# Attention and a gated feed-forward for one token: two weight loads cut into three transfers each by partitions

## The chip, the cores and the metric

One Trainium2 chip, one core of it. The metric is the time of the program on the device in microseconds (us), as a median of several executions. Beside it there is one profiled execution, which gives the trace. All times "at x us" are counted from the start of the profile's span.

## What is computed

One token `x` (512 values, bf16) goes through two branches that are mixed by a gate:

```python
g = sigmoid((x * gate_w).sum(-1, keepdims=True))
a = A_ref(x, k_cache, v_cache, wq, wo)   # attention, 32 query heads, 8 KV heads,
                                         # 32768 cached positions, head size 128
b = (silu(x @ w_gate) * (x @ w_up)) @ w_down     # 512 -> 1792 -> 512
return g * a + (1 - g) * b
```

`A_ref` projects `x` with `wq` (512 x 4096), takes scores against all cached keys of the KV head, softmax, the weighted sum of the values, and projects with `wo` (4096 x 512). The two caches hold 64 MiB each; with the weights some 148 MB have to be read once.

## The kernel before, in words

**Pages.** SBUF holds five pages of 32 KB per partition (`page`, L155). A cache page is half the positions of one KV head: 16384 positions x 128 values, 128 positions on each partition, 4 MB in one transfer of 128 partitions x 32,768 bytes. Keys use pages 0 and 2 (`PG_K`), values 1 and 3 (`PG_V`). Page 4 first holds `wq`, and at the end `wo`. Page 3 (`PG_F`) first holds `w_gate` and `w_up` side by side (`wgu`, L200): 128 partitions, for each weight four rows of 1792 values, which is 14,336 bytes per partition and weight.

**Queue.** All loads are issued by SyncE (SP) on one DMA queue (q1), in the order written out in its block (L259 to L312): `wq` (L279), the two rows of 1 KB (`x` L280, `gate_w` L281), `w_gate` and `w_up` (L283, in a loop over both), key pages 0 and 1 of the first head, value page 0, and from there on keys and values in turn (L262). Before a page is loaded again, SP waits until its reader is done: `sem_fill` for keys (L269), `sem_v_free` for values (L274). The second value page of the first head goes where the two weights lie, so SP waits there for `sem_pe_h` (L276), which TensorE (PE) raises after it has read the weights. At the end come the last value pages, `w_down` (L305) and `wo` in five transfers cut along its rows (L300).

A transfer raises its semaphore by 16 in all when it has landed, in parts as the DMA engines (16 of them) finish their shares. `sem_f` belongs to `w_gate` and `w_up` together: PE waits for 32 (L354).

**TensorE.** After the wait for `x` and the projection with `wq` (L334, 128 matmuls), PE waits for `sem_f` and multiplies both weights with `x` (L358, 112 matmuls). Then a loop over heads: for each key page, eight units of eight 128x128 transposes into PSUM (L372), copies by VectorE (L637), and score matmuls (L384); values of the head before are multiplied with the exponentials between (L429). ScalarE takes the exponentials (L540) after GpSimd's maximum over partitions (L254). At the end `w_down` and `wo` are multiplied with the results (L441, L453), the row is copied out of PSUM (L682), and SP and ScalarE store one half each, two rows of 256 bytes (L205).

**What the change touches**: the loop at L282 to L285 and the number in the wait at L354. The lines that the prediction's steps touch besides are L262 (page loads), L276 (SP's wait for PE), L358 and L372 (PE's work behind the wait), and L300, L453 and L682 (the end).

Of the kernel before, what the change touches and what calls it, by code (L numbers as in the profile page):

```python
# [13 lines left out]
def bass_gated_mix__gqa_block_cached__swiglu_ffn__decode_kernel(  # L14
# [23 lines left out]
    KC = D // 128  # L38
# [20 lines left out]
    WO_CUTS = [0, 8, 18, 26, 30, 32]  # L59
    KW = 1  # L60
    WD_CUT = 8
    WIDE = WO_CUTS[KW + 1]
    OC = NOUT // 128

# [12 lines left out]
    with ExitStack() as es:  # L77
        def S_(name):
            return es.enter_context(nc.semaphore(name))
# [3 lines left out]
        sem_f = S_("s_f")  # L83
# [46 lines left out]
        def T(name, shape, dt):  # L130
            return es.enter_context(nc.sbuf_tensor(name, shape, dt))
# [40 lines left out]
        O2 = T("O2", [128, WOJ], BF16)  # L172
        O2z = T("O2z", [128, WOJ - WIDE, SW], BF16)
        part = T("part", [128, NOUT], FP32)
# [25 lines left out]
        wgu = page[:, PG_F, 0 : 2 * KC * F].rearrange("p (w c f) -> p w c f", w=2, c=KC)  # L200
        wo_v = page[:, PG_X, 0 : WOJ * NOUT].rearrange("p (j n) -> p j n", j=WOJ)

        def store(eng, k):
            n = RPS * 128
            eng.dma_start(  # L205
                out[0, 0, n * k : n * (k + 1)].rearrange("(c n) -> c n", c=RPS),
                res_row[64 * k + SW - 1 : 64 * k + SW + 1, :],
            ).then_inc(sem_out, 16)

        with nc.Block("main") as block:  # L210
# [48 lines left out]
            @block.sync  # L259
            def _(sp):  # L260
                def cache(which, g, b, p, sem):
                    sp.dma_start(  # L262
                        page[:, p, :].rearrange("p (r d) -> p r d", d=DH),
                        which[0, g, b * BLK : (b + 1) * BLK, :].rearrange("(p r) d -> p r d", r=R),
                    ).then_inc(sem, 16)

                def load_k(g, b):
                    if g:
                        sp.wait_ge(sem_fill, UPG * (g - 1) + UPP * (b + 1))  # L269
                    cache(A_k_cache, g, b, PG_K[b], sem_page[PG_K[b]])  # L270

                def load_v(g, b):
                    if g:
                        sp.wait_ge(sem_v_free, NB * (g - 1) + b + 1)  # L274
                    elif PG_V[b] == PG_F:
                        sp.wait_ge(sem_pe_h, 1)  # L276
                    cache(A_v_cache, g, b, PG_V[b], sem_page[PG_V[b]])

                sp.dma_start(wq_v, A_wq.rearrange("(p c) n -> p c n", c=KC)).then_inc(sem_q, 16)  # L279
                sp.dma_start(x_row[0:1, :], A_x[0, :, :]).then_inc(sem_ld_x, 16)  # L280
                sp.dma_start(gw_row[0:1, :], gate_w.unsqueeze(0)).then_inc(sem_ld_x, 16)  # L281
                for w, src in enumerate((B_w_gate, B_w_up)):  # L282
                    sp.dma_start(  # L283
                        wgu[:, w, :, :], src.rearrange("(p c) f -> p c f", c=KC)
                    ).then_inc(sem_f, 16)  # L285
                for b in range(NB):
                    load_k(0, b)
                load_v(0, 0)
                load_k(1, 0)
                load_v(0, 1)  # L290
                load_k(1, 1)
                for g in range(2, G):
                    for b in range(NB):
                        load_k(g, b)
                        load_v(g - 1, b)

                def load_wo(k):
                    a, b = WO_CUTS[k], WO_CUTS[k + 1]
                    src = A_wo.rearrange("(p j) n -> p j n", j=WOJ)
                    sp.dma_start(wo_v[:, a:b, :], src[:, a:b, :]).then_inc(sem_wo[k], 16)  # L300

                load_v(G - 1, 0)
                sp.wait_ge(sem_fill, UPG * (G - 1) + UPP)
                cache(A_v_cache, G - 1, 1, PG_K[0], sem_page[PG_K[0]])
                sp.dma_start(  # L305
                    wd[:, :, :], B_w_down.rearrange("(p j) n -> p j n", j=FC)
                ).then_inc(sem_ld_wd, 16)
                sp.wait_ge(sem_pe_q, 1)
                for k in range(len(sem_wo)):
                    load_wo(k)  # L310
                sp.wait_ge(sem_dve_row, 1)
                store(sp, 0)  # L312

            @block.tensor
            def _(pe):
                pe.wait_ge(sem_ld_x, 32)
                pe.wait_ge(sem_const, 1)
                for src, base in ((x_row, M_X0), (gw_row, M_X0 + KC)):
                    srcv = src[0:1, :].rearrange("o (p c) -> o c p", c=KC)
# [31 lines left out]
                    )  # L351
                ins.then_inc(sem_pe_qp, 1)

                pe.wait_ge(sem_f, 32)  # L354
                for w, base in enumerate((M_G0, M_U0)):
                    for j in range(FC):
                        for c in range(KC):
# [81 lines left out]
                def emit_wide(w, vec, j, first, last):  # L439
                    c = j % NSTRIP  # L440
                    return pe.matmul(  # L441
                        ps_w[32 * c : 32 * c + 1, :],
                        vec[:, j : j + 1],
                        w[:, j, :],
                        start=first,
                        stop=last,
                        skip_group_check=True,
                    )

                def emit_rows(lhs, rhs, first, last):  # L450
                    for oc in range(OC):
                        e = oc % RPS
                        ins = pe.matmul(  # L453
                            ps_c[32 * oc : 32 * oc + (1 if e else SW), 0:128],
                            lhs(e),
                            rhs[:, oc * 128 : (oc + 1) * 128],
                            start=first,
                            stop=last,
                            skip_group_check=True,
                        )  # L460
                    return ins

                def emit_end():
# [11 lines left out]
                    pe.wait_ge(sem_psw, 1)  # L475
                    for j in range(WD_CUT):
                        emit_wide(wd, tT, j, j < NSTRIP, False)
# [5 lines left out]
                    for k, s in enumerate(sem_wo):  # L483
                        if k == 1:
                            for j in range(WD_CUT, FC):
                                emit_wide(wd, tT, j, False, False)
                        pe.wait_ge(s, 16)
                        for j in range(WO_CUTS[k], WO_CUTS[k + 1]):
                            if j < WIDE:
                                ins = emit_wide(wo_v, O2, j, False, j >= WIDE - NSTRIP)  # L490
                            else:
                                ins = emit_rows(
                                    lambda e: O2[:, j : j + 1] if e else O2z[:, j - WIDE, :],
                                    wo_v[:, j, :],
# [70 lines left out]
            def _(dve):  # L565
# [67 lines left out]
                with dve.Fori(0, G * STEP, STEP) as i:  # L633
# [42 lines left out]
                dve.tensor_copy(  # L676
                    O2z[:, :, SW - 1], ps_m[:, M_O0 + WIDE : M_O0 + WOJ]
                ).then_inc(sem_dve_oz, 1)
# [32 lines left out]
```

## Time and profile before

| what | us |
|---|---|
| time, median of 3 runs (range) | 352.69 (352.42 to 352.89) |
| the profiled execution | 352.48 |
| its span, first to last instruction | 350.7 |
| PE busy | 269.5 (77%) |
| VectorE (DVE) busy | 176.9 (50%) |
| ScalarE (ACT) busy | 32.1 (9%) |
| q1, share of 16 DMA engines | 98.5% |
| read from HBM | 148.11 MB, 422 GB/s over the span |
| `w_gate`, issue to landing | 15.4 |
| `w_up`, issue to landing | 20.6 |
| K pages, issue to landing (median) | 27.2 |

How to read it: the shares of busy time are averages over the whole span. The page has a line with the busy tenths of the DMA engines in 40 slices, one with GB/s, and one for each queue. The view of waits names the engine that waited, for whom, us in total, times and the longest. The chain of work is followed backwards from the last instruction, and each step names what released it. The timeline lists instructions of one line merged, with the idle time before them and what ended it. Beside these views the trace keeps a record of every DMA packet (queue, start, duration, bytes; not which of the 16 DMA engines) and of every increment that a landing transfer gives to its semaphore.

### The profile page before, as it was taken

Reading aid. Unit: us, or ns where it says so; the run is one execution under the profiler, and the core shown is the slowest. Engines: PE = TensorE matmul, PEld = TensorE weight load, DVE = VectorE, ACT = ScalarE, POOL = GpSimd, SP = SyncE. Lnnn points to the kernel's source line nnn. Section 1 sums busy time; section 2 is a strip of 40 time slices with the busy share of each in tenths; the row PEclk is TensorE's granted clock in tenths of the full one; section 3 lists DMA queues with packets and bytes.
Section 4 is the critical chain, followed back from the end, with each engine's and each line's share of the span. In section 5 each row is a group of like instructions: output and inputs, shape, how many; then the busy total and the mean of one; then the engine's idle time right before and its main releaser. Section 6 shows DMA issues by size and latency. Waiting matters only on the chain.

```text
span 350.7 us, 8919 instructions
## 1 busy us (share of the span) xinstructions
PE 269.5 (77%) x4005; PEld 232.4 (66%) x4005; DVE 176.9 (50%) x193; ACT 32.1 (9%) x148; POOL 6.9 (2%) x29
## 2 busy tenths in 40 slices
PE   0446987898999959796797949696898959795584
PEld 0446987887796939495785839394876849493232
DVE  0010878474783928365472828175653819184011
ACT  1000000500030040002100040003000040004000
POOL 4000000000000000000000000000000000000000
PEclk9999989696998999889696989679886969679565
DMA  8999999999999999999999999999999999999995
GB/s 329 418 448 417 437 430 439 418 430 426 445 434 422 430 431 441 430 430 422 445 434 426 430 426 445 430 426 426 441 437 426 426 430 445 430 426 426 422 419 218
DMA packets 5925, 148.25 MB, mean 423 GB/s; under 512 B 666, under 2 KB 668, under 8 KB 924
## 3 DMA queue, kind: packets, MB, share of 16 engines
q1 hardware_dynamic: 5912, 148.12, 98.5%
q8 instruction: 7, 0.11, 0.1%
q14 instruction: 2, 0.02, 0.0%
q10 hardware_dynamic: 4, 0.00, 0.0%
HBM read 148.11 MB, written 0.00 MB: 422 GB/s over the span
## 4 chain that ended last, share of the span: by engine, by line
DMA 64%; PE 31%; DVE 2%; SPq 1%; issue 1%
DMA page<-in_A_k_cache_dram 53%; PE pst L372 23%; DMA page<-in_A_wo_dram 11%; PE ps_sc L384 5%; DVE ktT L637 2%; PE ps_o L429 1%; PE pst L453 1%; PE pst L441 0%; PE ps_m L410 0%; SPq L283 0%; SPq L262 0%; DVE part L680 0%; SPq L305 0%; SPq L300 0%; SPq L279 0%
## 5 line engine op out<-in xcount | busy, mean ns | idle before, releaser
L637 DVE COPY ktT<-pst 128x2048 bf16<-128x2048 bf16 x128 | 156.1, 1224 | 106.5 <-PE pst L372 99.4
L372 PE MATMUL pst<-ident_f,page 128*128 128x128 f32 x1024 | 160.2, 315 | 40.2 <-DMA page<-in_A_k_cache_dram 38.8
L372 PEld LDWEIGHTS pst<-ident_f,page 128*128 128x128 f32 x1024 | 137.2, 164 | 50.6 <-DMA page<-in_A_k_cache_dram 46.7
L384 PEld LDWEIGHTS ps_sc<-qcur,ktT 128*128 128x128 bf16 x2048 | 67.0, 97 | 11.4 <-DVE ktT L637 10.0
L384 PE MATMUL ps_sc<-qcur,ktT 128*128 128x8 bf16 x2048 | 67.9, 166 | 8.6 <-DVE ktT L637 8.6
L429 PE MATMUL ps_o<-page,ET 128*16 128x512 bf16 x512 | 42.1, 487 | 4.6 <-DMA page<-in_A_v_cache_dram 4.6
L429 PEld LDWEIGHTS ps_o<-page,ET 128*16 128x16 bf16 x512 | 13.3, 104 | 23.2 <-issue 10.7
L531 ACT ACTIVATE nbias<-gmax 128x4 f32<-128x4 f32 x8 | 1.6, 205 | 263.6 <-POOL gmax L254 263.6
L540 ACT ACTIVATE ET<-ps_sc,nbias 128x128 bf16<-128x128 f32 x64 | 23.9, 554 | 0.6
L540 ACT ACTIVATION_READ_ACCUMULATOR ET<-ps_sc,nbias 128x1 f32 x64 | 18.2, 284 | 0.0
L642 DVE TENSOR_REDUCE pmaxf<-ps_sc 128x4 f32<-128x512 f32 x16 | 11.1, 691 | 11.5 <-PE ps_sc L384 11.5
L410 PE MATMUL ps_m<-sel,acc 128*128 128x4 f32 x72 | 10.8, 273 | 3.7 <-ACT acc L552 3.7
L410 PEld LDWEIGHTS ps_m<-sel,acc 128*128 128x128 f32 x72 | 10.1, 217 | 4.3 <-ACT acc L552 4.3
L358 PE MATMUL ps_m<-xT,page 128*128 128x1 bf16 x112 | 6.9, 198 | 4.8 <-DMA page<-in_B_w_up_dram 4.8
L321 PE MATMUL ps_m<-ones_bf,x_row 1*128 1x1 bf16 x4 | 0.3, 174 | 13.1 <-DMA gw_row<-in_gate_w_dram 13.1
L358 PEld LDWEIGHTS ps_m<-xT,page 128*128 128x128 bf16 x112 | 6.8, 162 | 4.9 <-DMA page<-in_B_w_up_dram 4.9
L254 POOL PARTITION_ALL_REDUCE gmax<-pmax x8 | 3.0, 373 | 302.7 <-DVE pmax L644 302.7
L321 PEld LDWEIGHTS ps_m<-ones_bf,x_row 1*128 1x128 bf16 x4 | 0.2, 116 | 13.1 <-DMA gw_row<-in_gate_w_dram 13.1
L552 ACT ACTIVATE acc<-ps_o 128x512 f32<-128x512 f32 x8 | 5.2, 653 | 13.6 <-PE ps_o L429 13.6
L660 DVE RECIPROCAL rS<-pst 128x32 f32<-128x32 f32 x1 | 0.4, 359 | 12.1 <-PE pst L465 12.1
L577 DVE CAST xT<-ps_m 128x4 bf16<-128x4 f32 x1 | 0.2, 163 | 12.1 <-PE ps_m L321 12.1
L616 DVE TENSOR_TENSOR t<-sg,ps_m 128x14 f32<-128x14 f32 x1 | 0.2, 170 | 10.7 <-ACT sg L525 10.7
(65 smaller groups left out, 38.4 us busy)
## 6 DMA issues: line engine op xcount, KB each, us to landing
page<-in_A_k_cache_dram SPq DMA_DIRECT2D x16, 4096.0 KB, 27.2
page<-in_A_v_cache_dram SPq DMA_DIRECT2D x16, 4096.0 KB, 31.1
page<-in_A_wq_dram SPq DMA_DIRECT2D x1, 4096.0 KB, 12.2
page<-in_A_wo_dram SPq DMA_DIRECT2D x2, 1024.0 KB, 38.8
page<-in_B_w_gate_dram SPq DMA_DIRECT2D x1, 1792.0 KB, 15.4
page<-in_B_w_up_dram SPq DMA_DIRECT2D x1, 1792.0 KB, 20.6
wd<-in_B_w_down_dram SPq DMA_DIRECT2D x1, 1792.0 KB, 34.5
page<-in_A_wo_dram SPq DMA_DIRECT2D x1, 1280.0 KB, 39.1
```

The costliest lines, as they stand in the source:

```text
L254: pool.partition_all_reduce(gmax[:, g, :], pmax[:, g * STEP : g * STEP + HPG], 128, ReduceOp.max).then_inc(sem_gmax, 1)
L358: ins = pe.matmul(ps_m[:, base + j : base + j + 1], wgu[:, w, c, :].rearrange("d (p j) -> d j p", j=FC)[:, j, :], xT[:, c : c + 1], start= ...
L372: ins = pe.transpose(pst[u % NST][:, k * 128 : (k + 1) * 128], kv[:, n * 128 : (n + 1) * 128], ident_f[:, :],)
L384: ins = pe.matmul(ps_sc[b][:, col : col + 2 * HPG], kt[:, k, e, :], qcur[:, e, :], start=(e == 0), stop=(e == 1),)
L410: ins = pe.matmul(ps_m[:, M_P0 : M_P0 + HPG], acc[:, q, :], sel4[:, q * HPG : (q + 1) * HPG], start=(q == 0), stop=(q == RQ - 1),)
L429: ins = pe.matmul(ps_o[32 * c : 32 * c + RQ * HPG, :], ET[:, n : n + RQ, :].rearrange("p n h -> p (n h)"), view[:, k * RQ : (k + 1) * RQ, ...
L453: ins = pe.matmul(ps_c[32 * oc : 32 * oc + (1 if e else SW), 0:128], lhs(e), rhs[:, oc * 128 : (oc + 1) * 128], start=first, stop=last, sk ...
L531: act.activation(nbias[:, g, :], gmax[:, g, :], ACT.Copy, scale=-SCALE).then_inc(sem_nbias, 1)
L540: act.activation(ET[:, b * R : (b + 1) * R, h], sc[:, h, :], ACT.Exp, bias=nbias[:, g, h : h + 1], scale=SCALE, accum_out=esum[:, g, b, h ...
L552: act.activation(acc[:, :, :].rearrange("p q d -> p (q d)"), ps_o[:, :], ACT.Copy).then_inc(sem_acc, STEP)
L637: dve.tensor_copy(ktT[:, u % NKT, :], pst[u % NST][:, :].bitcast(BF16)).then_inc(sem_cp, 1)
L642: dve.tensor_reduce(pmaxf[:, b, :], sc, AX.X, ALU.max).then_inc(sem_pmax, 4)
```

## The change

Each of the two weights is loaded in three transfers instead of one, cut by partitions: `w_gate` in 0 to 111, 112 to 123 and 124 to 127 (112, 12 and 4 partitions), `w_up` in 0 to 111, 112 to 119 and 120 to 127 (112, 8 and 8). They stand in the same place in SP's order, the bytes of each partition and their destination are the same, and each transfer raises `sem_f` by 16, so PE waits for 96 instead of 32. Nothing else changes.

```diff
+    FFN_CUTS = ((0, 112, 124, 128), (0, 112, 120, 128))
...
                 for w, src in enumerate((B_w_gate, B_w_up)):
-                    sp.dma_start(
-                        wgu[:, w, :, :], src.rearrange("(p c) f -> p c f", c=KC)
-                    ).then_inc(sem_f, 16)
+                    srcv = src.rearrange("(p c) f -> p c f", c=KC)
+                    for a, b in zip(FFN_CUTS[w], FFN_CUTS[w][1:]):
+                        sp.dma_start(wgu[a:b, w, :, :], srcv[a:b, :, :]).then_inc(sem_f, 16)
...
-                pe.wait_ge(sem_f, 32)
+                pe.wait_ge(sem_f, 16 * sum(len(c) - 1 for c in FFN_CUTS))
```

One line is added near the top, and the loop keeps its length, so that a line of the changed kernel is one further down than in the kernel before (L358 is L359); the loads of the two weights are at L286.

## The prediction

> **What bounds the kernel now.** I read the page from its second part down: the slices, the queues, the chain. Then the waits, the windows and the timeline, and last the records behind them, of single DMA packets and landings.
>
> From the page: the busy tenths and rates of the DMA queues, the queue that carries the data, and the chain that ended last.
>
> ```profile
> DMA  8999999999999999999999999999999999999995
> GB/s 329 418 448 417 437 430 439 418 430 426 445 434 422 430 431 441 430 430 422 445 434 426 430 426 445 430 426 426 441 437 426 426 430 445 430 426 426 422 419 218
> ...
> q1 hardware_dynamic: 5912, 148.12, 98.5%
> q8 instruction: 7, 0.11, 0.1%
> ...
> DMA 64%; PE 31%; DVE 2%; SPq 1%; issue 1%
> ```
>
> The transfers never pause. 148.12 MB go through q1 at one rate, and PE's 31% of the chain lies between DMA landings that released it.
>
> The waits (us in total, times, longest) say the same: PE waits for K pages, hardly for anything else.
>
> ```profile
> PE pst L372 <- DMA page<-in_A_k_cache_dram: 38.8, 13, 4.6
> ...
> PE ps_m L358 <- DMA page<-in_B_w_up_dram: 4.8, 1, 4.8
> ```
>
> The last windows column is GB/s, the one before it the DMA share:
>
> ```profile
> 103.00:303.00 200.00, 164.06 (x2424) 141.88 (x2422) 111.85 (x110) 18.08 (x90) 1.86 (x5) 0.84 1.00 432
> ```
>
> 432 over 16 is 27.0 GB/s for one DMA path (one of the 16 engines with its ring). The packet records refine this: each path starts a 32,768 B packet every 1.210 us and a 14,336 B packet every 0.532 us, to some ns, from the fifth packet of a path to the end. These are 27.1 and 26.9 GB/s. When one path stalls the others do not speed up: **the limit is per path, not one pool.** A path that falls behind stays behind.
>
> How far apart they are, the landing records tell: the last w_o transfer's sixteen increments come from 346.17 to 348.15 us. Against the first, eight paths lie at 0 to 0.53, two at 0.89 and 1.04, six at 1.59 to 1.98 us. The cause is in the packet records: six paths stood for 0.93 to 1.09 us each, while a 16 KB instruction packet (q8) went through, and two others for 0.31 us (8 KB). The latest path sets the end; the last matmul starts at 348.19, and the last copy follows:
>
> ```profile
> 304.64 39.11 DMA page<-in_A_wo_dram
> ...
> 348.65 0.29 DVE res_row L682
> ```
>
> The span is 350.7 us and this execution's time 352.48, so 1.78 us lie around it; the median of the runs shown is 352.69, 0.21 more. I add to 352.48.
>
> **The change, part by part.** Bytes, partitions and matmuls stay. What changes is which path writes which row (one row is 14,336 B for one partition). Before, 128 rows are 8 for each path, twice: 16. How are small transfers spread? The packet records have two cases: the x row and the gate row (one partition) are one 1,024 B packet each, both on the same path, and a store of two partitions is two packets starting 5 ns apart, hence on two. So I take an even division and the same paths first: 112 rows as 16x7, 12 as 12x1, 4 as 4x1, 8 as 8x1. Call the paths 0 to 15. Rows for both weights: paths 0 to 3 get 7+1+1+7+1+1 = 18; 4 to 7 get 7+1+7+1+1 = 17; 8 to 11 get 15; 12 to 15 get 14. By the count alone that is +1.06, +0.53, -0.53 and -1.06 us (rows by 0.532). The trace does not number its paths: of 0 to 3 only the x row's path is known to be an early one.
>
> *Issue on SP.* Two issues of 0.36 and 0.53 us become six. Four more by 0.23 to 0.53 (SP's rows of the head) are 0.9 to 2.1, say 1.5 us, by which the first K issue moves from 2.79. Cost 0: q1 is busy with w_q until 12.4 us. Without that cover it would cost the 1.5. There are 32 more semaphore packets (16+12+4+16+8+8 = 64 for 32) of 9 ns, at most 4 more on a path: 0.04 us.
>
> *PE's wait* is one wait as before, now for 96. Behind it stand the 112 matmuls of L358 and then the K transposes:
>
> ```profile
> 22.84 6.88 PE L358 MATMUL ps_m<-xT,page 128*128 128x1 bf16 x112 [4.84 <-DMA page<-in_B_w_up_dram]
> ...
> 32.86 5.16 PE L372 MATMUL pst<-ident_f,page 128*128 128x128 f32 x24 [3.13 <-DMA page<-in_A_k_cache_dram]
> ```
>
> If the weights land late, so does the K page behind them on the same rings, and the 3.13 us of idleness between the two groups stay about as they are. The V load that waits for sem_pe_h stands on SP behind a K load issued at 44.62, 15 us after the matmuls end. Cost 0 beside the path's own delay.
>
> *The rows themselves.* Here lies the price. In every transfer of before, a path writes eight partitions that no other path writes, so the trace cannot say whether the 27 GB/s belong to the path or to the partitions it writes to. The change separates them: four transfers put 12, 4, 8 and 8 paths on the last 16 partitions, which are two paths' worth of rows by any even share. Lower bound: sharing costs nothing, a row is 0.532. Upper: the partitions of one share take 27 GB/s whoever writes; with four paths in one share a row takes 4x0.532 = 2.13 us, with eight 4.26. I take **four to a share**, the smaller reading, between the ends; the rows nearest to it are the instruction packets: through the same paths, to another destination, 16 KB took 0.946 to 1.107 us, 15 to 17 GB/s. A path's pace depends on where it writes.
>
> Paths 0 to 3 then need 14x0.532 + 4x2.13 = 15.97 us where they needed 16x0.532 = 8.51: +7.5. Shares of seven rows do not line up with shares of eight either, so in each 112-row transfer a path meets another about once: one row doubled, 2x0.53 = +1.1 (from 0 to twice that). The share's own path, ahead by then with its K page, writes there too: a fifth writer for part of the four rows, estimated at half of 4x0.53, or +1.1 (from 0 to 2.1). Sum +9.7 on the slowest of paths 0 to 3. The end is set by the latest path, and these may have had a lead of up to 1.98; with eight of sixteen late I take off 1.2. **Net +8.5: 352.48 + 8.5 = 361.0 us.** Small readings of all three (7.5 - 1.98) give 358.0, large ones (7.5+2.1+2.1) 364.2. Eight to a share wherever more than four rows go: three rows at 4.26, one at 2.13, 7.45+14.9-8.5 = +13.9, the far end, 366.4.
>
> [...]
>
> **The rivals.**
> 1. *The pace belongs to the path, and the late paths are 8 to 15* (not slower). For it: identical pace whatever the size or source. Against: nothing ever tried two writers. The late ones shed 0.53 or 1.06; the first four arrive at no later than about 0.53+1.06 = 1.6 instead of 1.98: -0.4, 352.1 us. It needs early paths at 0 to 3 and decides only if sharing costs them under 0.4 us in all.
> 2. *The pace belongs to the path, but a late one is among the first four:* 1.98+1.06, so +1.1, 353.5 us. Eight late paths of fifteen make this as likely as the first, if they do not lie in a row.
> 3. *Sharing is partial*, as when a share takes two writers at full pace: a row 1.06, four rows +2.1, two extra rows +1.06 included in the count: 14x0.532+4x1.06-8.51 = +3.2, with meetings up to +5: 356 us.
> 4. *The 112 rows go out one row to each path in turn*, so that all sixteen stand on two or four shares at once: 14 rows at 2.13 are 30 for 7.5, over +20: 375 us.
>
> That the change does nothing at all is excluded unless small transfers are spread over all sixteen paths; the two small cases above speak against it.
>
> **How the numbers follow.** Forecast 0.70, rivals 0.13, 0.07, 0.07 and 0.03. The forecast gets most since a path's pace was seen to change with its destination, and since the change puts four writers and more where only one ever wrote; rivals 1 and 2 share 0.20 because the even pace is explained by the path as well. Under 0.2% (0.7 us) this kernel cannot be told from no change. Faster by that: 0.03, as perfect evenness of the sixteen (mean 1.0 behind the first, latest 1.98) is worth only 1.0 us. Within: 0.12, the rest of the first rival and some of the second. Slower: 0.85. The range, 353.0 to 365.0, holds rivals 2 and 3 and the forecast but for its far end: 8 in 10.
>
> **What would show it.** q1 with 5944 packets; w_up's landing (22.8 us before) at 30 to 33 and the first K page (32.8) at 41 to 43, the sixteen increments of a K page then spread over 6 us or more instead of 2; everything after it shifted by about 8.5, with PE's waits for K pages unchanged in sum to some us. A first K page at 33 to 34 with the old spread means rivals 1 or 2, and I am wrong on sharing; w_up past 45 means rival 4. Rows of 14,336 B with 2.1 us in the packet records prove the step, rows of 0.53 disprove it.

## The result, and the profile after

The changed kernel takes 363.62 us (median of 6, 362.84 to 364.67), the kernel before 352.61 (median of 6): a ratio of 1.0315, 95% interval 1.0304 to 1.0326, or **+11.0 us**. The forecast was slower, 361.0 in 353.0 to 365.0. The profiled execution has a span of 361.8 us, 11.1 more than before. Of the executions behind this document one, of the near kernel below, took 1136.2 us and is left out of its ratio.

The page of the changed kernel, the lines that answer to those shown of before: DMA slices and rates, the queue, the chain.

```profile
DMA  8999999999999999999999999999999999999993
GB/s 344 318 219 288 422 433 429 429 427 428 442 420 442 420 438 428 435 428 435 435 424 438 424 438 428 435 428 438 431 424 442 424 442 420 435 431 435 416 417 159
...
q1 hardware_dynamic: 5944, 148.12, 98.2%
...
DMA 65%; PE 30%; DVE 2%; SPq 1%; issue 1%
```

The busy line is as full as before, and so is q1's share. The line below tells the two kernels apart: slices 2 to 4 move 318, 219 and 288 GB/s where they moved 418, 448 and 417. So a path counts as busy also while its bytes move at half the rate (the windows below have a share of 1.02 at 216 GB/s). From slice 5 on the rates are the old ones.

The windows view of the changed kernel puts that in stages (last two columns: DMA share, GB/s).

```profile
12.10:17.50 5.40, 3.99 (x136) 3.83 (x136) 0.92 (x6) 0.20 (x1) 0.39 (x1) 1.00 1.03 295
17.50:33.00 15.50, 0.21 (x2) 0.14 (x2) 1.23 (x6) 0.00 (x0) 0.00 (x0) 1.00 1.02 216
33.00:43.00 10.00, 7.04 (x113) 6.96 (x114) 0.40 (x2) 0.18 (x1) 0.00 (x0) 1.00 1.00 428
103.00:303.00 200.00, 161.13 (x2413) 141.27 (x2412) 112.86 (x113) 21.76 (x108) 2.23 (x6) 0.86 1.00 432
```

The first row is the first 112-partition transfer, the second the rest of the weights, half of the usual 432. The long stretch in the middle has the same 432 as before: what is lost is lost by about 33 us (but for 1.0 us on the latest path, below), and it is never won back.

TensorE in the timeline: the matmuls with the two weights start at 33.40 instead of 22.84, and the first K page 9.99 later than before. Between the two PE idles 2.56 us (3.13 before), so the late weights cost nothing beside the delay of the page behind them.

```profile
33.40 6.89 PE L359 MATMUL ps_m<-xT,page 128*128 128x1 bf16 x112 [15.47 <-DMA page<-in_B_w_up_dram]
...
42.85 4.38 PE L373 MATMUL pst<-ident_f,page 128*128 128x128 f32 x24 [2.56 <-DMA page<-in_A_k_cache_dram]
```

In the view of waits, K pages cost PE 42.0 us (38.8 before), and the wait for `w_up` has grown from 4.8 to 15.5.

```profile
PE pst L373 <- DMA page<-in_A_k_cache_dram: 42.0, 13, 5.6
...
PE ps_m L359 <- DMA page<-in_B_w_up_dram: 15.5, 1, 15.5
```

The chain ends with the same steps, 11 us later:

```profile
315.53 39.32 DMA page<-in_A_wo_dram
...
359.71 0.29 DVE res_row L683
```

The records of packets and landings give the sum. The 256 rows of the two weights take 15.97 us on the mean path (8.59 before). The K-page packets that start up to 70 us have 2.56 us over their usual 1.213 on the mean path (0.30 before). That is +7.4 and +2.3, together +9.6. The last `w_o` transfer's sixteen landings have a mean of 356.80 us (347.12 before, +9.7). The latest lies 2.41 behind that mean, before 1.03: another +1.4. 9.7 + 1.4 = 11.1.

Of the latest path's 11.1, some 1.0 has another source. At the landing of the first K page it is 10.0 us later than before (42.81 for 32.82). The sixteen landings of a page are 3.16 us apart in the one that ends at 71.96 us, and 4.18 in the one that ends at 82.69; between them, at 69.05, stands a 16 KB instruction packet of 1.09 us. Before, the landings of a page stay about 2.0 us apart. So an instruction packet met the path that was already the latest.

### The profile page after: what moved, and what is told of

Same layout as the page of the kernel before. It is cut to its first block, busy times and chain, and to the rows that moved or that the text cites. A ratio compares the mean times of both kernels' runs of the same rounds, so it can differ in the third digit from the quotient of the medians.

```text
span 361.8 us, 8923 instructions
## 1 busy us (share of the span) xinstructions
PE 266.0 (74%) x4005; PEld 229.3 (63%) x4005; DVE 176.8 (49%) x193; ACT 32.1 (9%) x148; POOL 6.9 (2%) x29
## 4 chain that ended last, share of the span: by engine, by line
DMA 65%; PE 30%; DVE 2%; SPq 1%; issue 1%
DMA page<-in_A_k_cache_dram 54%; PE pst L373 23%; DMA page<-in_A_wo_dram 11%; PE ps_sc L385 5%; DVE ktT L638 2%; PE ps_o L430 1%; PE pst L454 1%; SPq L286 1%; PE pst L442 0%; PE ps_m L411 0%; SPq L263 0%; DVE part L681 0%; SPq L306 0%; SPq L301 0%; SPq L280 0%
## 5 line engine op out<-in xcount | busy, mean ns | idle before, releaser
L373 PE MATMUL pst<-ident_f,page 128*128 128x128 f32 x1024 | 157.9, 312 | 43.9 <-DMA page<-in_A_k_cache_dram 42.0
L373 PEld LDWEIGHTS pst<-ident_f,page 128*128 128x128 f32 x1024 | 134.6, 162 | 54.5 <-DMA page<-in_A_k_cache_dram 50.3
L430 PE MATMUL ps_o<-page,ET 128*16 128x512 bf16 x512 | 39.8, 465 | 6.8 <-DMA page<-in_A_v_cache_dram 6.7
L359 PE MATMUL ps_m<-xT,page 128*128 128x1 bf16 x112 | 6.9, 198 | 15.5 <-DMA page<-in_B_w_up_dram 15.5
L643 DVE TENSOR_REDUCE pmaxf<-ps_sc 128x4 f32<-128x512 f32 x16 | 11.1, 692 | 11.5 <-PE ps_sc L385 11.5
L359 PEld LDWEIGHTS ps_m<-xT,page 128*128 128x128 bf16 x112 | 6.8, 163 | 15.6 <-DMA page<-in_B_w_up_dram 15.6
```

Of the source, the lines that this page charges most:

```text
L359: ins = pe.matmul(ps_m[:, base + j : base + j + 1], wgu[:, w, c, :].rearrange("d (p j) -> d j p", j=FC)[:, j, :], xT[:, c : c + 1], start= ...
L373: ins = pe.transpose(pst[u % NST][:, k * 128 : (k + 1) * 128], kv[:, n * 128 : (n + 1) * 128], ident_f[:, :],)
L430: ins = pe.matmul(ps_o[32 * c : 32 * c + RQ * HPG, :], ET[:, n : n + RQ, :].rearrange("p n h -> p (n h)"), view[:, k * RQ : (k + 1) * RQ, ...
L643: dve.tensor_reduce(pmaxf[:, b, :], sc, AX.X, ALU.max).then_inc(sem_pmax, 4)
```

## The experiments

Theory S, that of the forecast: a path has 27 GB/s (432 over 16), but a group of partitions has only that too, and paths that write to the same group divide it. The rivals: theory C, that only the number of rows on a path counts; F, that transfers on fewer than 16 paths are slow in themselves; N, that the number of transfers or the wait costs the time. In this section a difference is that of the medians (for near that of the ratio), the interval that of the ratio. The extra rows are told apart from those of `w_up` by following each path: a packet starts within some 30 ns of the end of the one before it. The kernel before was run beside each (352.5 to 352.6 us).

### Neighbouring or distant partitions

Two kernels, each the kernel before with four small transfers behind `w_up` (ahead of the first K page). They load rows of `w_down` into `wd`, which is loaded again at the end; SP waits for them before that. Both read the same rows of HBM and differ in the partitions that they write to.

```diff
+                wdv = B_w_down.rearrange("(p j) n -> p j n", j=FC)
+                for e, f in EXT:
+                    sp.dma_start(wd[e, :, :], wdv[f, :, :]).then_inc(sem_ext, 16)
...
 near:  EXT = tuple((slice(4*i, 4*i + 4), slice(4*i, 4*i + 4)) for i in range(4))
 apart: EXT = tuple((slice(i, 16 + i, 4), slice(4*i, 4*i + 4)) for i in range(4))
```

Near:

> The kernel before, with four more transfers behind w_up: 4 neighbouring partitions each (0 to 3, 4 to 7, 8 to 11, 12 to 15) of w_down, 14,336 bytes per partition, into the place that w_down fills again later. By the even division, paths 0 to 3 get four rows more each. Theory S: four paths write to one share of partitions, a row takes 2.1 us in the packet records, the four rows 8.5 us: +6.5 to +8.5 us, less up to 2.0 for a lead of these paths. Theory C: a row takes 0.53, four rows 2.1 us: +0.1 to +2.1. Theory F: as theory S.

Apart:

> As the run with four neighbouring partitions: the same rows of w_down are read, by four transfers of four rows, but each transfer writes to partitions four apart (0, 4, 8, 12; then 1, 5, 9, 13; and so on). Theory S: four different shares, a row takes 0.53 us: +0.1 to +2.1 us in all. Theory C: the same. Theory F: a row takes 2.1 us, +6.5 to +8.5 as with neighbours.

Near took 357.13 to 358.61 us, ratio 1.0151 (1.0125 to 1.0176), +5.3; apart 353.81, 1.0033 (1.0020 to 1.0045), +1.2. The sixteen rows of the near kernel have a mean of 1.06 us and a longest of 1.83; those of the other 0.535, each of them. The windows of the two show it, near first:

```profile
20.90:22.80 1.90, 0.00 (x0) 0.00 (x0) 0.00 (x0) 0.00 (x0) 0.00 (x0) 1.00 0.86 189
```

```profile
20.90:22.80 1.90, 0.00 (x0) 0.00 (x0) 0.00 (x0) 0.00 (x0) 0.00 (x0) 1.00 0.97 414
```

The reader sees the same stretch with the same queued work, at 189 and at 414 GB/s. Same bytes, same sources, four paths each: only the destination differs. F and C fall. The near price is below the 6.5 to 8.5 that S expected. Four paths at 0.535 in lockstep would be 2.14 for a row, and none took over 1.83; why the mean is half of it, no run here shows. The +1.2 of the distant rows is the count alone: four rows are 2.1 us, so paths 0 to 3 had a lead of about 0.9 (0.5 to 1.4 by the interval).

But S in this form does not give the 189 GB/s. Twelve paths have no extra row; at 27 GB/s each they alone would move 324. The packet records show what S lacks. Eleven of these paths went on from `w_up` to the K page as the extra rows began; their first packet of the K page took 2.03 to 2.27 us, against 1.21 or 1.22 in the apart kernel, although four groups can be the own groups of four paths at most. So while some paths share, paths that write elsewhere are slowed as well. How that comes about, no run here shows.

### How many rows the big part costs

One transfer more behind `w_up`, of 112 partitions or of all 128, in the same way.

```diff
+                EXT = ((slice(0, 112), slice(0, 112)),)
...
+                EXT = ((slice(0, 128), slice(0, 128)),)
```

112 partitions:

> The kernel before with one more transfer behind w_up: partitions 0 to 111 of w_down into the place that w_down fills again later, seven rows for each path. Theory S, with seven rows of a path not lining up with the shares: the rows behind the first take 0.8 to 0.9 us, 5.5 us in all: +5 to +6 us. Theory C: 7 x 0.532 = +3.7 us.

128 partitions:

> The kernel before with one more transfer of all 128 partitions of w_down behind w_up, eight rows for each path: the control for the run with 112 partitions, which took seven rows and came out 8.1 us above before. Theories S and C: each path writes its own partitions, rows of 0.53 us, +4.3 us. If the extra load costs something beside its rows (HBM, the later wait on SP), it is more than 4.5 us here too, and the 8.1 of the other run are not the sharing's.

112 partitions: 360.71 us, 1.0228 (1.0211 to 1.0245), **+8.1**. 128 partitions: 356.77, 1.0122 (1.0105 to 1.0139), **+4.3**. Fewer bytes take nearly twice as long. The 112 rows have a mean of 0.86 us, and they are slow on every path; the 128 rows have 0.535 and none above 0.546. The control is at its count of rows to 0.1 us, so an extra load costs nothing but its rows. S expected +5 to +6 for 112, and the rows themselves are +6.0 (from 20.9 to 26.9 us in the records of most paths). The rest comes behind them: the first 32 packets of the K page take 1.56 us instead of 1.21, on paths that are done while others still write their extra rows.

### Two halves, and 120 partitions

```diff
+                EXT = ((slice(0, 64), slice(0, 64)), (slice(64, 128), slice(64, 128)))
...
+                EXT = ((slice(0, 120), slice(0, 120)),)
```

> The same 128 rows of w_down as the control, in two transfers of 64 partitions (0 to 63 and 64 to 127): four rows for each path twice, eight in all as in the control. Theory S with shares of four neighbouring partitions alone: a path has four neighbours to itself, rows of 0.53 us, +4.3 us. [...] Theory C: +4.3 us.

> The kernel before with one more transfer behind w_up, partitions 0 to 119 of w_down: by an even division fifteen paths with eight rows each, as many per path as in the control with 128 partitions, which took +4.3 us. [...] Theory S with whole shares for whole paths, as in the control: +4.3 us. Theory C: +4.3 us.

The halves: 363.17 us, 1.0299 (1.0282 to 1.0317), +10.7, against +4.3 for the same 128 rows in one transfer; S with four neighbours to a share, and C, give +4.3 for them too. 120 partitions: 363.75, 1.0309 (1.0280 to 1.0337), +11.2, where S with whole shares for whole paths, and C, give +4.3. The rows take 1.07 and 1.09 us, twice 0.535. The windows over the extra rows, of the one transfer with 128 and then of the halves:

```profile
20.80:25.00 4.20, 1.88 (x31) 1.88 (x32) 0.00 (x0) 0.00 (x0) 0.00 (x0) 1.00 1.02 434
```

```profile
20.80:25.00 4.20, 0.00 (x0) 0.00 (x0) 0.00 (x0) 0.00 (x0) 0.00 (x0) 1.00 1.05 218
25.00:29.00 4.00, 3.25 (x54) 3.25 (x55) 0.00 (x0) 0.00 (x0) 0.00 (x0) 1.00 1.06 228
```

434 GB/s becomes 218, what eight paths of 27 GB/s carry (216), though by the even division each of sixteen paths has four rows. S does not give this with groups of four neighbours: every path of a half then has a group to itself. With eight neighbours to a group it would, but the apart run excludes that: there four paths wrote partitions four apart, each at full pace (0.535 us a row). So either partitions that are not neighbours are in one group, or paths slow each other in another way; which, these runs do not tell. Beyond the doubled rows (8 rows at 1.07, +8.6) the K page pays again: its first 32 packets take 1.71 us instead of 1.21.

### The parts of the change

`w_gate` alone cut, `w_up` alone cut, and both cut at 112 only:

```diff
-    FFN_CUTS = ((0, 112, 124, 128), (0, 112, 120, 128))
+    FFN_CUTS = ((0, 112, 124, 128), (0, 128))
...
+    FFN_CUTS = ((0, 128), (0, 112, 120, 128))
...
+    FFN_CUTS = ((0, 112, 128), (0, 112, 128))
```

> Only w_gate is cut (112, 12 and 4 partitions), w_up is loaded whole. The change took 11.0 us for both. Theory S: the 112 rows at 0.85 instead of 0.53 are +2.2 us on every path, the rows on 12 and 4 partitions 1.3 to 2.1 us each for paths 0 to 3 instead of the one row that they replace: +5 to +6.5 us. Theory C (9 rows instead of 8 on paths 0 to 3, less their lead): 0 to +0.5 us.

> Only w_up is cut (112, 8 and 8 partitions), w_gate is loaded whole. Theory S: +5 to +6.5 us as for w_gate, and the two parts together about the 11.0 us of the change. Theory C (9 rows instead of 8 on paths 0 to 7): 0 to +0.5 us.

> Both weights are cut at 112 only, into 112 and 16 partitions: every path gets 7 + 1 rows for each weight, 16 in all, as before the change. Theory S (a path shares the pace of the partitions it writes to with the other paths that write there): each of the two 16-partition rows takes about 2.1 us instead of 0.53, +3.2 us on every path, and the two 112-row transfers take about 5.5 us instead of 3.7, +3.5: about +6.7 us against before, 358 to 361. Theory C (only the number of rows on a path counts): no change within 0.5 us. Theory F (transfers on fewer than 16 paths are slow in themselves, whatever they write): no change either, since all four transfers use 16 paths.

`w_gate` alone: 357.74 us, 1.0145 (1.0128 to 1.0162), +5.2. `w_up` alone: 357.99, 1.0156 (1.0139 to 1.0173), +5.5. Together 10.7 of the 11.0: the parts add, and the paths are full in both (a DMA share of 0.98 to 1.20 in the windows from 12.3 to 26.0 us). Both at 112 only: 359.45, 1.0194 (1.0173 to 1.0216), +6.9 at 16 rows on each path, the old count. So C fails here as well, and F too, since all four transfers use 16 paths, and over 6 of the 11 us come without any change in the number of rows.

### As many transfers, but of all partitions

```diff
-    FFN_CUTS = ((0, 112, 124, 128), (0, 112, 120, 128))
+    FFN_CUTS = ((0, 2, 3, 4), (0, 2, 3, 4))
...
-                        sp.dma_start(wgu[a:b, w, :, :], srcv[a:b, :, :]).then_inc(sem_f, 16)
+                        sp.dma_start(wgu[:, w, a:b, :], srcv[:, a:b, :]).then_inc(sem_f, 16)
```

> Three transfers for each weight as in the change, and PE waits for 96, but cut along the four rows of 1792 values of each partition (2, 1 and 1 of them): every transfer spans all 128 partitions and every path writes eight of them, as before the change. Theory S: no sharing, rows at the old pace, +0 to +0.3 us for 64 more packets on each path. Theory N (the number of transfers, SP's six issues or the wait for 96 cost the time): near the +11.0 us of the change.

The number of packets rises by 36 on each path, not by 64 (q1 has 6488 for 5912). 352.84 us, ratio 1.0010 (1.0001 to 1.0020): +0.3 us (0.0 to 0.7), and N falls. Six transfers, six issues and the wait for 96 are together within 0.7 us; it is the cut by partitions that costs.

## Why the prediction was right, and where it was off

- *What bounds the kernel*: right. Sixteen full paths, no catching up: 432 GB/s in the middle in both kernels. The mean landing is 9.6 us later than before at the first K page and 9.7 at the end; the latest path's delay alone grew, from 10.0 to 11.1.
- *Issue and wait at nothing*: right. The first K issue went from 2.79 to 4.18 (1.4 where 1.5 was estimated) behind the cover of `w_q`; the run cut along the rows bounds all of it at 0.7 us. The 32 more semaphore packets are there: q1 has 5944.
- *The V load that waits for PE*: right. SP waits for K pages to be read the same 14 times, 224.8 us for 213.6, and the 11.2 more are the delay itself (its longest wait, 48.5 for 40.3, holds most of it).
- *The rows, four to a share*: that paths which write to the same few partitions slow each other was right, shown by near against apart (1.06 us a row against 0.535). The slow instruction packets that it was inferred from (0.946 to 1.107 us for 16 KB) did not show it, since they stand in another queue too (q8 for q1). That four to a share make a row of 4x0.532, 2.13 us, was an estimate, and no run shows a share of that size: with four paths on neighbouring partitions the near run has rows of 1.06 us on the mean and 1.83 at most. Rows of up to 2.15 us stand in the records of the changed kernel, 30 of them over 1.5.
- **The mis-sized terms.** "In each 112-row transfer a path meets another about once", +1.1 for both, was too small. The first 112 rows took 0.80 us on the mean, +1.9 for one transfer, and it is every path that pays. "4x2.13" on paths 0 to 3, 8.5 us, was too large: in the near run four such rows cost 5.3, with the lead of 0.9 some 6.2. In the changed kernel one path with 18 rows can be followed through all of them: the four on the last 16 partitions took 0.90, 1.96, 1.89 and 1.82 us, 6.6 for the 8.5, and the fourteen others 11.8 us, where 14x0.532 and the 1.1 for meetings make 8.5. These errors went in opposite directions, so that the sum (+9.7 before the lead) lay as near as it did is in part luck.
- *A fifth writer on the K page*, +1.1: the K page paid +2.3 on the mean path. The reason given was too narrow, since in the near run eleven paths without an extra row pay as well (2.03 to 2.27 us for a packet of 1.21).
- *The lead of 1.2 taken off*: the distant rows show a lead of about 0.9 on paths 0 to 3. But the idea behind it failed, since it was thought that paths 8 to 15 go free and run ahead. The first landing of the end moved by 8.9 us and the latest by 11.1, so all paths were slowed, and they came out further apart. One path with 14 rows, none of them on the last 16 partitions, took 13.2 us for them instead of 14x0.532, 7.4.
- *What would show it*: the first K page at 42.85 was inside 41 to 43. `w_up` landed at 33.35, just past the 30 to 33. A spread of 6 us or more over a K page's sixteen increments was wrong: the first page has 3.2, for the same reason.
- *The rivals*: the first two, pace by path alone, fall to near against apart. The third, +3.2 to +5 with four writers at 1.06 a row, is too small for the +11.0, and the path followed above took 1.82 to 1.96 us for three of its four rows. The fourth (+20) did not come. The first would also have had little to give: four rows more without sharing already cost 1.2 us, so paths 0 to 3 are not early by the 1.5 us that it counted on.

Open: which partitions each path takes in a 112-partition transfer. The records do not number paths or partitions; an even division into seven neighbours for each path, with groups of four, is an estimate, and by it some rows would be slow, but not all sixteen paths equally (0.86 us on the mean). The near run says that a path need not have an extra row to be slowed (2.03 to 2.27 us for 1.21); by what it is slowed then stays open, and so how the 11 us divide between paths that write to the same partitions and paths that do not. And whether the source in HBM adds anything in the 112 and 120 cases was not tried apart from the destination.

## What to carry to other kernels

Where the DMA queue is the bound, as here (q1 at 98%), cut transfers along the free dimension and leave all 128 partitions in each: the same number of transfers cost 0.3 us that way and 11 the other way. Dividing evenly over 16 paths is not enough, as 64 and 112 partitions show (1.07 and 0.86 us a row for 0.535). To price such a cut, ask for every path and every moment who else writes to neighbouring partitions (near and apart: +5.3 and +1.2 us), expect the other paths to be slowed too (2.03 to 2.27 us a packet for 1.21), and add what the transfer behind it pays on the same paths (2.3 us beside 7.4 here). And read GB/s by slice beside the busy line: paths that slow each other look busy (a share of 1.02 at 216 GB/s).

## What the runs showed of the hardware beyond what was expected

- 64 partitions at a time ran at 218 to 228 GB/s and 120 partitions at rows of 1.09 us, against 434 and 0.535 for 128 in one transfer.
- The K page behind slowed transfers is slowed too: its first 32 packets took 1.76 (near), 1.56 (112 partitions) and 1.71 us (halves) instead of the 1.21 of the kernel before, and 2.39 in the changed kernel.
- Paths beside those that write to neighbouring partitions are slowed with them: eleven paths without an extra row took 2.03 to 2.27 us for a K packet in the near kernel, 1.21 or 1.22 in the apart kernel.
- The pace is even to some ns when one transfer takes all 128 partitions: of its 128 extra rows none was outside 535 to 546 ns.
